# Attention and mixture-of-experts on one core: moving the tiny addition ahead of the softmax reciprocal from GpSimd to VectorE, from the third attention stage on

## The chip, the cores and the metric

One core of one Trainium2 chip. The metric is the device time of one execution in microseconds (us). The profile shows TensorE as PE (matmuls) and PEld (weight loads), VectorE as DVE, ScalarE as ACT, GpSimd as POOL, and SyncE, which issues the DMAs here, as SP.

## What is computed

```python
scores = scale * np.matmul(q, k.transpose(0, 1, 3, 2))     # 4 batches, 8 heads, 576 x 576, head size 64
kth = np.partition(scores, -32, axis=-1)[..., -32:-31]
scores = np.where(scores >= kth, scores, -1e9)
attn = np.exp(scores - scores.max(-1, keepdims=True))
attn = attn / (attn.sum(-1, keepdims=True) + 1e-09)
x = attn @ v                                                # laid out as 2304 rows of 512
P = np.exp(x @ w_gate - max)                                # 2304 x 8, eight rounds of row and column scaling
out = sum(P[:, e:e+1] * (np.maximum(x @ w1[e], 0) @ w2[e]) for e in range(8))
```

All in float32. The `1e-09` in the fifth line is the addition that the change moves.

## The kernel before, in words

The program has two halves that run interleaved on the same engines. Attention goes through the seven entries of `STAGES`; an entry is a batch with one or two blocks of 256 query rows, over four pairs of heads. The expert layer is computed for blocks of rows as soon as their attention is done, and its matmuls (lines 446 and 559) fill TensorE while attention goes on. When all attention is done, `sinkhorn` scales the gate matrix, and the last four blocks are computed together from line 671 and line 730 on.

One attention step of a head pair goes as follows. TensorE computes scores (lines 122 and 123) into one PSUM tile; ScalarE copies them to `s` (line 128); VectorE finds the 32 largest of each row by four maxima and three replacements (lines 138 and 141); GpSimd subtracts two of these numbers (line 142, `eb`); ScalarE raises the kept weights with two activations (lines 144 and 145), the second of which adds up the row sums into `st`. Then `normalise` runs: GpSimd adds 1e-9 to the sums (line 171), VectorE takes the reciprocal (line 172), and GpSimd (line 175) or ScalarE (line 177) multiplies the weights `Et` by it. Two row tiles of two heads go into one `st` of 128x2; the mixed rests of two batches (`rest_weights`) have an `st` of 128x1.

From the third stage on the weights are turned by a DMA: ScalarE splits `Et` into 16-bit halves (line 158, `halves`), SP transposes them (line 162, `turned`), and ScalarE joins them into `at` (line 165). The join is put in the program behind the next split, not behind its own. TensorE then multiplies `at` by the values (line 247; "the weigh" below: ten instructions in the program, twenty in the trace), and ScalarE copies the result to `xt` (line 270).

The expert layer splits each weight tile into a high part (`wh`, ScalarE, line 83) and a low part (`wl`, GpSimd, line 86), multiplies (line 446), stores the hidden layer as `hh` (ScalarE, line 514) and `hl` (VectorE, line 515), and multiplies again (line 559).

Nobody wrote the order of the instructions out: a list scheduler places every instruction in its engine's queue by priority (attention before experts) and by its own estimate of when the operands are there. Each engine then runs its queue strictly in that order. So an edit of one line can change the order of everything behind it. In `normalise`, `X` is the dictionary of finished row tiles: it has 2 entries in the first stage, 4 in the second and 6 in the third.

Of the kernel before, what the change touches and what calls it, by code (L numbers as in the profile page):

```python
# [11 lines left out]
OP = mybir.AluOpType  # L12
# [39 lines left out]
def kernel(  # L52
# [11 lines left out]
    nc = tc.nc  # L64
# [49 lines left out]
    X = {}  # L114
# [53 lines left out]
        turning.append(whole)  # L168

    def normalise(Et, st, n, on_pool=False):  # L170
        nc.gpsimd.tensor_scalar(st[:, 0, 0:n], st[:, 0, 0:n], 1e-9, 1.0, op0=OP.add, op1=OP.mult)
        nc.vector.reciprocal(st[:, 1, 0:n], st[:, 0, 0:n])
        for i in range(n):
            if on_pool:
                nc.gpsimd.tensor_scalar(Et[:, i, :], Et[:, i, :], st[:, 1, i:i + 1], 1.0, op0=OP.mult, op1=OP.mult)
            else:
                nc.scalar.activation(Et[:, i, :], Et[:, i, :], AF.Copy, scale=st[:, 1, i:i + 1])
# [41 lines left out]
    def weight_tiles(qs, ks, put, on_pool=False, crossed=None):  # L219
        for t in range(2):  # L220
            Et = ap_.tile([128, 2, S], F32, name="Et", bufs=2)
            st = ap_.tile([128, 2, 2], F32, name="st", bufs=3)
            units = []
            for i in range(2):
                o = i * 256 + t * 128
                qc = qs[:, o:o + 128]
                sp = scores([((a, 0, 288), [(qc, ks[i], slice(a * 288, a * 288 + 288))]) for a in range(2)])
                units.append((copy_scores(sp[:, :, 0:288]), Et[:, i, :], st[:, 0, i:i + 1]))
            topk(units, crossed is not None)
            normalise(Et, st, 2, on_pool)  # L230
            cs = slice(t * 128, (t + 1) * 128)
            if crossed is not None:
                cross(Et, crossed[:, :, cs])
                continue
            Ef = Et.rearrange("p a b -> p (a b)")
            for g in range(3):
                ps = pst.tile([128, 4, 128], F32, name="pt")
                for r in range(3):
                    j = g * 3 + r
                    nc.tensor.transpose(ps[:, r, :], Ef[:, j * 128:j * 128 + 128], idt)  # L240
                put(slice(g * 3, g * 3 + 3), cs, ps[:, 0:3, :])
# [37 lines left out]
    def rest_weights(qm, ks, put):  # L279
        Et = ap_.tile([128, 2, S], F32, name="Et", bufs=2)  # L280
        st = ap_.tile([128, 2, 2], F32, name="st", bufs=3)
        qa, qb = qm[:, 0:128], qm[:, 128:256]
        sp = scores([
            ((0, 0, 288), [(qa, ks[0], slice(0, 288)), (qb, ks[1], slice(64, 352))]),
            ((1, 0, 224), [(qa, ks[0], slice(288, 512)), (qb, ks[1], slice(352, 576))]),
            ((1, 224, 288), [(qa, ks[0], slice(512, 576)), (qb, ks[1], slice(0, 64))]),
        ])
        topk([(copy_scores(sp[:, :, 0:288]), Et[:, 0, :], st[:, 0, 0:1])])
        normalise(Et, st, 1)
        ps = pst.tile([128, 4, 128], F32, name="pt")  # L290
        for j in range(4):
            nc.tensor.transpose(ps[:, j, :], Et[:, 0, j * 128:(j + 1) * 128], idt)
        for i in range(2):
            put(slice(0, 128), slice(5 * i, 5 * i + 4), ps[:, :, i * 64:(i + 1) * 64])
        ps = pst.tile([128, 4, 128], F32, name="pt")
        nc.tensor.transpose(ps[0:64, 0, :], Et[:, 0, 512:576], idt)
        nc.tensor.transpose(ps[:, 1, :], Et[:, 0, 448:576], idt)
        for i, r in enumerate((va, vb)):
            put(r, 4, ps[r, i, r])
# [536 lines left out]
```

## Time and profile before

| | |
|---|---|
| median of 3 runs | 1862.87 us (1862.12 to 1863.7) |
| the profiled execution | 1861.39 us, of which its span is 1859.6 us |
| PE busy in the span | 1794.2 us, 96% |
| DVE, ACT, POOL busy | 65%, 63%, 56% |
| attention's last `normalise` (line 172) | at 1012.1 us |

Read the share of PE first: it is the engine that both halves need all the time. Then ask in which stretch the rest of its time lies; the profile's 40 slices show it mostly in the first eighth of the span.

### The profile page before, as it was taken

To read this page: it belongs to the slowest core of one execution; us is meant where nothing else is said; L and a number is where in the kernel's file an instruction comes from. 1 tells how busy PE (TensorE), PEld (TensorE's weight loads), DVE (VectorE), ACT (ScalarE), POOL (GpSimd) and SP (SyncE) were. 2 spreads that over 40 slices of the span, in tenths; PEclk is the share of its full clock that TensorE was granted. 3 is DMA by queue.
4 is the path that set the end of the run, shared out by engine and by line. 5 is a ranking of instruction groups with operands and counts; after the bars stand their busy time and mean duration, and the time that the engine had idled before them with its cause. 6 is when DMAs were issued, how large, how long until landed. Compare 5 with 4: busy or idle time off the path is not lost.

```text
span 1859.6 us, 26250 instructions
## 1 busy us (share of the span) xinstructions
PE 1794.2 (96%) x9361; PEld 1484.4 (80%) x9361; DVE 1208.9 (65%) x2235; ACT 1172.1 (63%) x1773; POOL 1047.8 (56%) x827
## 2 busy tenths in 40 slices
PE   4899998999999999999999999999999999999998
PEld 3778787878877878878877788888888888888886
DVE  8989988888888886978965231145555555533433
ACT  5888889898988987898888435433333333333331
POOL 3369755655655547565643948945554455555441
PEclk8999999999999999999999999999999999999999
DMA  4787766666556656565554337523333333311111
GB/s 128 237 286 237 218 173 186 203 169 165 165 144 167 173 135 198 155 160 162 165 134 112 105 131 227 185 85 111 117 110 117 103 102 108 97 62 59 56 35 45
DMA packets 212674, 266.17 MB, mean 143 GB/s; under 512 B 127424, under 2 KB 131648, under 8 KB 212544
## 3 DMA queue, kind: packets, MB, share of 16 engines
q1 hardware_dynamic: 212544, 264.51, 48.0%
q8 instruction: 73, 1.20, 0.3%
q14 instruction: 57, 0.47, 0.1%
HBM read 201.54 MB, written 34.60 MB: 127 GB/s over the span
## 4 chain that ended last, share of the span: by engine, by line
PE 73%; ACT 7%; DVE 6%; issue 5%; DMA 5%; POOL 4%; SPq 0%; ACTq 0%; POOLq 0%; DVEq 0%
PE p L730 19%; PE p L559 15%; PE p L446 14%; PE p L671 9%; PE pc L671 5%; DMA wr<-in_w_dram 3%; PE pt L247 3%; DVE m L138 3%; POOL wl L86 2%; PE pb L671 2%; DVE w L141 2%; PE sp L122 2%; PE sp L123 2%; ACT wh L83 1%; ACT at L165 1%
## 5 line engine op out<-in xcount | busy, mean ns | idle before, releaser
L86 POOL TENSOR_TENSOR wl<-wr,wh 128x1024 fp32r<-128x1024 f32 x280 | 675.1, 2420 | 509.9 <-ACT wh L83 500.1
L83 ACT ACTIVATE wh<-wr 128x1024 fp32r<-128x1024 f32 x280 | 295.1, 1060 | 281.9 <-PE p L671 191.6
L138 DVE MAX8 m<-w 128x8 f32<-128x576 f32 x432 | 321.8, 754 | 6.5
L446 PE MATMUL p<-xh,wh 128*128 128x256 f32 (+1 forms) x800 | 270.3, 338 | 1.5 <-DVE hl L515 1.5
L446 PE MATMUL p<-xh,wl 128*128 128x256 f32 (+1 forms) x800 | 268.4, 336 | 0.0
L446 PE MATMUL p<-xl,wh 128*128 128x256 f32 (+1 forms) x800 | 268.4, 335 | 0.0
L559 PE MATMUL p<-wh,hh 128*128 128x512 f32 x640 | 251.2, 397 | 4.7 <-ACT hh L514 4.5
L559 PE MATMUL p<-wl,hh 128*128 128x512 f32 x640 | 249.2, 392 | 0.0
L559 PE MATMUL p<-wh,hl 128*128 128x512 f32 x640 | 239.5, 391 | 0.0
L141 DVE MATCH_REPLACE8 w<-m,w 128x576 f32<-128x576 f32 x288 | 213.8, 743 | 0.0
L515 DVE SCALAR_TENSOR_TENSOR hl<-p,hh 128x512 fp32r<-128x512 f32 x160 | 109.0, 683 | 148.0 <-ACT hh L514 146.3
L730 PE MATMUL p<-wh,h2h 128*128 128x512 f32 x512 | 199.4, 389 | 1.3 <-ACT h2h L694 0.7
L730 PE MATMUL p<-wl,h2h 128*128 128x512 f32 x512 | 199.2, 389 | 0.0
L730 PE MATMUL p<-wh,h2l 128*128 128x512 f32 x512 | 196.4, 389 | 0.0
L576 DVE SCALAR_TENSOR_TENSOR acc<-p,P,acc 128x512 f32<-128x512 f32 x120 | 89.4, 749 | 160.9 <-PE p L730 160.9
L446 PEld LDWEIGHTS p<-xh,wh 128*128 128x128 f32 x800 | 152.4, 190 | 21.4 <-DVE hl L515 3.1
L446 PEld LDWEIGHTS p<-xh,wl 128*128 128x128 f32 x800 | 152.3, 190 | 15.7 <-issue 0.8
L446 PEld LDWEIGHTS p<-xl,wh 128*128 128x128 f32 x800 | 152.3, 190 | 15.5
L138 DVE MAX8 m<-s 128x8 f32<-128x576 f32 x144 | 108.2, 752 | 76.0 <-ACT s L128 75.3
L559 PEld LDWEIGHTS p<-wh,hh 128*128 128x128 f32 x640 | 120.6, 189 | 30.3 <-ACT hh L514 7.1
L559 PEld LDWEIGHTS p<-wl,hh 128*128 128x128 f32 x640 | 120.7, 189 | 23.0 <-POOL wl L86 0.2
L559 PEld LDWEIGHTS p<-wh,hl 128*128 128x128 f32 x640 | 119.8, 188 | 23.8 <-issue 0.4
(168 smaller groups left out, 3551.8 us busy)
## 6 DMA issues: line engine op xcount, KB each, us to landing
wr<-in_w_dram SPq DMA_DIRECT2D x240, 512.0 KB, 3.5
y<-y SPq DMA_DIRECT2D x160, 256.0 KB, 2.7
raw<-in_k_dram SPq DMA_DIRECT2D x56, 288.0 KB, 3.8
raw<-in_q_dram SPq DMA_DIRECT2D x32, 256.0 KB, 3.7
p<-y SPq DMA_DIRECT2D x32, 256.0 KB, 3.5
wr<-in_w_dram SPq DMA_DIRECT2D x32, 256.0 KB, 4.0
y<-p SPq DMA_DIRECT2D x32, 256.0 KB, 3.8
values<-in_v_dram SPq DMA_DIRECT2D x28, 256.0 KB, 3.1
```

The lines of the kernel that those rows point to most:

```text
L83: nc.scalar.activation(dst, src, AF.Copy)
L86: nc.gpsimd.tensor_tensor(dst, src, hi.bitcast(F32), op=OP.subtract)
L122: nc.tensor.matmul(o, qc, kh[:, cs], start=(i == 0), stop=False)
L138: nc.vector.max(m8[:, u, r, :], ws[u] if r else units[u][0])
L141: nc.vector.match_replace(ws[u], m8[:, u, r, :], ws[u] if r else units[u][0], LOWEST)
L247: weighed = nc.tensor.matmul(av[r, 0:n], vr[:, o:o + 64], at[:, block, 0:n], start=(j == order[0]), stop=(j == order[-1]))
L446: nc.tensor.matmul(ps[:, fo, :], a[:, kk, fs], x[:, k0 + kk, cs], start=(i == 0), stop=(i == 3 * nk - 1))
L515: nc.vector.scalar_tensor_tensor(seat.hl[:, ft, cs], src, 0.0, seat.hh[:, ft, cs].bitcast(F32), op0=OP.max, op1=OP.subtract)
L559: nc.tensor.matmul(ps, a[:, ft, ts], m[:, ft % 2, :], start=(i == 0), stop=(i == 3 * NFT - 1))
L576: return nc.vector.scalar_tensor_tensor(ACC[t], y, g, ACC[t], op0=OP.mult, op1=OP.add)
L671: nc.tensor.matmul(ps, w[:, kk, :], x[:, kk, :], start=(fresh and i == 0), stop=(i == 5), skip_group_check=True)
L730: nc.tensor.matmul(ps, a[:, ft, ts], m[:, ft, :], start=(i == 0), stop=(i == 11))
```

## The change

For every call of `normalise` in the third stage and behind it, the addition of 1e-9 is issued on VectorE, the engine that takes the reciprocal next. In the first two stages it stays on GpSimd. 64 of the 80 additions move: 48 of 128x2 and 16 of 128x1.

```diff
     def normalise(Et, st, n, on_pool=False):
-        nc.gpsimd.tensor_scalar(st[:, 0, 0:n], st[:, 0, 0:n], 1e-9, 1.0, op0=OP.add, op1=OP.mult)
+        adder = nc.vector if len(X) > 4 else nc.gpsimd
+        adder.tensor_scalar(st[:, 0, 0:n], st[:, 0, 0:n], 1e-9, 1.0, op0=OP.add, op1=OP.mult)
         nc.vector.reciprocal(st[:, 1, 0:n], st[:, 0, 0:n])
```

Behind the edit every line has a number higher by one, so line 172 of before is line 173 in the change, and the addition is line 172 there. The scheduler's order is the same up to the first moved addition and differs from there on all engines. Three places:

VectorE, at the first addition that moves, in the third stage (`m_1740` and `m_1809` are maxima of two row tiles). Before:

```order
L515 SCALAR_TENSOR_TENSOR hl<-p_3442,hh 128x2x256
L515 SCALAR_TENSOR_TENSOR hl<-p_3460,hh 128x2x256
L141 MATCH_REPLACE w<-m_1740,w 128x576
L138 MAX m_1809<-s 128x8
L138 MAX m_1740<-w 128x8
L172 RECIPROCAL st<-st 128x2
L141 MATCH_REPLACE w<-m_1809,s 128x576
```

With the change:

```order
L516 SCALAR_TENSOR_TENSOR hl<-p_3442,hh 128x2x256
L516 SCALAR_TENSOR_TENSOR hl<-p_3460,hh 128x2x256
L172 TENSOR_SCALAR st<-st 128x2
L141 MATCH_REPLACE w<-m_1740,w 128x576
L138 MAX m_1809<-s 128x8
L173 RECIPROCAL st<-st 128x2
L138 MAX m_1740<-w 128x8
L141 MATCH_REPLACE w<-m_1809,s 128x576
```

The addition stands two instructions ahead of the reciprocal, and the reciprocal one instruction earlier than before.

ScalarE, around the join (`at`) on which the eleventh weigh of the program waits (in the trace of before it starts at 300.84 us; `p_3917` is an expert result that is copied out just ahead). Before:

```order
L128 ACTIVATE s<-sp 128x576
L83 ACTIVATE wh<-wr 128x1024 x2
L144 ACTIVATE Et<-s,m_2145 128x576
L83 ACTIVATE wh<-wr 128x1024
L567 ACTIVATE y<-p_3917 128x512
L158 ACTIVATE halves<-Et 128x2304
L165 ACTIVATE at<-turned 128x9x256
L128 ACTIVATE s<-sp 128x576
L514 ACTIVATE hh<-p_3954 128x2x256
L514 ACTIVATE hh<-p_4011 128x2x256
```

With the change:

```order
L144 ACTIVATE Et<-s,m_2145 128x576
L568 ACTIVATE y<-p_3917 128x512
L515 ACTIVATE hh<-p_3976 128x2x256
L515 ACTIVATE hh<-p_3954 128x2x256
L128 ACTIVATE s<-sp 128x576
L83 ACTIVATE wh<-wr 128x1024 x2
L144 ACTIVATE Et<-s,m_2145 128x576
L158 ACTIVATE halves<-Et 128x2304
L165 ACTIVATE at<-turned 128x9x256
L128 ACTIVATE s<-sp 128x576
```

The store of `p_3954`, a copy of scores, a weight split and a weight activation (the second with `m_2145`) stood behind the join before and stand ahead of it now. Another split and another activation came in from ahead of the join in front, which changes nothing for this one.

TensorE, at the same weigh. Before:

```order
L446 MATMUL p_4011<-xh,wl 128x256
L122 MATMUL sp<-kh,qs 128x288
L123 MATMUL sp<-kl,qs 128x288
L122 MATMUL sp<-kh,qs 128x288
L123 MATMUL sp<-kl,qs 128x288
L247 MATMUL pt<-at,values 64x256 x10
```

With the change:

```order
L560 MATMUL p_4227<-wh,hh 128x512
L560 MATMUL p_4227<-wl,hh 128x512
L560 MATMUL p_4227<-wh,hl 128x512
L248 MATMUL pt<-at,values 64x256 x10
L122 MATMUL sp<-kh,qs 128x288
```

Between the weigh in front of this one and this one the queue holds 18 expert matmuls of line 446 and 48 of line 559 before, and 66 and 60 with the change.

Counted over TensorE's whole queue: at the thirteenth weigh and at the sixteenth (456.4 us in the trace) as many expert matmuls stand ahead as before, to within two. Between the sixteenth and the twenty-first weigh (629.36 us) there are 290 of line 446 and 324 of line 559 before, and 264 and 276 with the change. Ahead of the first matmul of `sinkhorn` there are 103 fewer. They are run behind it; the number of all matmuls is the same.

## Rows read from the trace of the kernel before

**Rows 1.** The page, part 1: busy time of each engine

```profile
PE 1794.2 (96%) x9361; PEld 1484.4 (80%) x9361; DVE 1208.9 (65%) x2235; ACT 1172.1 (63%) x1773; POOL 1047.8 (56%) x827
```

**Rows 2.** Busy time by stretch, first the stretch and its length

```profile
core 0: us, PE busy (x) PEld busy (x) DVE busy (x) ACT busy (x) POOL busy (x), PEclk, DMA share, GB/s
0.00:205.00 205.00, 166.31 (x959) 134.20 (x959) 192.21 (x403) 160.72 (x301) 121.69 (x120) 0.97 0.68 221
205.00:460.00 255.00, 239.15 (x1554) 204.35 (x1555) 223.82 (x441) 229.16 (x334) 149.41 (x138) 0.97 0.66 184
460.00:630.00 170.00, 169.09 (x859) 137.05 (x859) 139.68 (x273) 146.57 (x211) 97.43 (x85) 1.00 0.59 157
630.00:1012.00 382.00, 380.83 (x2038) 309.05 (x2033) 301.42 (x589) 327.32 (x492) 215.16 (x191) 1.00 0.57 157
```

**Rows 3.** Waits of PE from 205 to 1012: us, times, longest

```profile
PE pt L247 <- ACT at L165: 7.3, 2, 6.2
PE sp L122 <- ACT s L128: 6.2, 5, 1.9
```

**Rows 4.** PE timeline around 294 to 306: start, us, what, idle before

```profile
294.19 0.30 PE L122 MATMUL sp<-kh,qs 128*128 128x288 f32 x1
294.33 0.29 PE L123 MATMUL sp<-kl,qs 128*128 128x288 f32 x1
300.84 4.53 PE L247 MATMUL pt<-at,values 128*64 128x256 f32 x20 [6.22 <-ACT at L165]
305.31 0.61 PE L122 MATMUL sp<-kh,qs 128*128 128x288 f32 x1
...
306.43 0.52 PE L559 MATMUL p<-wh,hh 128*128 128x512 f32 x1
```

**Rows 5.** The stretch of 6 us behind that wait, columns as in rows 2

```profile
301.00:307.00 6.00, 6.00 (x26) 3.63 (x27) 5.54 (x11) 5.13 (x11) 3.51 (x4) 0.53 0.79 184
```

**Rows 6.** ACT timeline ahead of that weigh

```profile
288.31 0.76 ACT L145 ACTIVATE Et<-Et,eb 128x576 f32<-128x576 f32 x1
...
296.39 2.13 ACT L158 ACTIVATE halves<-Et 128x2304 uint16<-128x2304 uint16 x1
298.41 2.38 ACT L165 ACTIVATE at<-turned 128x2304 uint16<-128x2304 uint16 x1
```

**Rows 7.** Chain that ended last, two pieces: start, us, what

```profile
307.65 2.27 PE p L446 x19
...
338.91 5.47 PE p L559 x24
```

**Rows 8.** POOL's additions by shape: busy, mean ns, idle before

```profile
L171 POOL TENSOR_SCALAR st<-st 128x2 f32<-128x2 f32 x64 | 12.3, 192 | 64.8 <-ACT Et L145 61.9 <-POOL qs L86 0.2
...
L171 POOL TENSOR_SCALAR st<-st 128x1 f32<-128x1 f32 x16 | 3.1, 191 | 9.9 <-ACT Et L145 8.8
```

**Rows 9.** DVE timeline in the sinkhorn part: small instructions

```profile
1042.28 0.15 DVE L403 TENSOR_SCALAR nmx<-nmx 128x1 f32<-128x1 f32 x1
...
1043.29 0.18 DVE L414 TENSOR_SCALAR sp<-sp 128x18 f32<-128x18 f32 x1
1043.51 0.27 DVE L415 RECIPROCAL rs<-sp 128x18 f32<-128x18 f32 x1
```

**Rows 10.** Waits of DVE from 205 to 1012

```profile
DVE m L138 <- ACT s L128: 71.8, 40, 5.4
DVE st L172 <- POOL st L171: 23.8, 16, 4.8
```

**Rows 11.** Waits of POOL from 205 to 1012

```profile
POOL st L171 <- ACT Et L145: 49.3, 25, 6.4
```

**Rows 12.** The sixteenth weigh: ns min, median, max, first and last start

```profile
L247 PE MATMUL pt<-at,values x20: 432/432/483, 456.4 to 458.8; 128*64 128x320 f32 x20
```

**Rows 13.** PE timeline, the twenty-first weigh

```profile
629.36 2.38 PE L247 MATMUL pt<-at,values 128*64 128x256 f32 x20
```

**Rows 14.** ACT timeline, the join for that weigh

```profile
622.63 2.40 ACT L165 ACTIVATE at<-turned 128x2304 uint16<-128x2304 uint16 x1
```

## The prediction, made before the change was run

> **What bounds the kernel now.** I read the share of each engine first: PE is busy for 1794.2 of 1859.6 us [rows 1], so 65.4 us of the span are all that any better order can give back. Then the stretches [rows 2], to see where these 65.4 lie. The reader is to take length minus PE busy in each row: 38.7 us lie before 205, where the first two stages run and the order of every queue is unchanged; 15.85 lie between 205 and 460; 0.9 between 460 and 630; 1.2 between 630 and 1012; and the remaining 8.8 behind 1012, where attention is over. So the change can work on some 18 us. In the same rows VectorE is busy for 88% and ScalarE for 90% of 205 to 460, for 82% and 86% of 460 to 630, for 79% and 86% of 630 to 1012. GpSimd is never above 60%. In the first of the three stretches the attention chain is just about too slow for TensorE, in the other two TensorE is the bound and the chain has air.
>
> Then the waits of PE [rows 3]. One wait stands out: 6.2 us for the join of the turned weights. The timeline of PE [rows 4] shows it: the last score matmul starts at 294.33, the weigh at 300.84. On ScalarE the join starts at 298.41, at once behind the split of the next weights [rows 6]; ScalarE has been busy without a break since 288.31, so it is its queue that is late, not GpSimd's addition. The wait has an echo: in the 6 us behind it the granted clock is 0.53, mostly the lower of its two levels of 1.2 and 2.4 GHz [rows 5]. The weigh takes 4.53 us there [rows 4] against 2.38 for the same twenty instructions later [rows 13], 2.15 more. The four scores behind it take 1.12 (305.31 to 306.43) where a step is 0.14 otherwise (294.19 to 294.33), 0.56 more. The wait and its echo cost 6.2 + 2.7 = 8.9 us.
>
> **The instruction that moves.** GpSimd loses 64 additions of 192 and 191 ns [rows 8], 12.3 us, and the waits for the exponentials in front of them, 49.3 us in 25 cases [rows 11]. While it stood there, nothing behind it in its queue could start. Since GpSimd is idle 40% of the time and more, none of this is on the path that sets the end; I take 0 for it, covered by that idle time. VectorE gains 64 additions. Its trace has no 128x2 addition, so I bound it by near rows [rows 9]: a 128x1 multiplication took 0.15 us, and from a 128x18 addition to the dependent reciprocal behind it pass 0.22 us. That is 9.6 to 14.1 us; I take the upper one, because the moved addition too has a dependent reciprocal behind it, though mostly with two instructions in between. Against it stand the 23.8 us that VectorE waited at the reciprocal for GpSimd's addition [rows 10]. That wait doesn't vanish: VectorE now waits at its own addition for ScalarE's sums, in strict order, with the maxima of the next row tile queued behind. What goes is only GpSimd's 0.19 and its queue ahead of it. Below, nothing is gained; above, all of the 23.8; in sum I put VectorE's balance at zero, with -14 and +10 as ends, spread over 800 us.
>
> A page of the Trainium skill has a lower price: GPSIMD Engine Reference, section 8 (Key points), holds VectorE to be about twice as fast as GpSimd in elementwise work. By it an addition would be 96 ns (an estimate from that ratio and the 192 ns of the row) and all of them 6.1 us, and VectorE's share in the tight stretch below would come out about one point lower. The rows on VectorE's small instructions do not bear that out, 0.15 to 0.18 us against 0.19, and I go by them.
>
> **The order.** This is where the time is decided. At the late weigh TensorE's queue now holds 48 more matmuls of line 446 and 12 more of line 559 between the weigh in front and this one. A step of the former is 2.27/19 = 0.119 us, of the latter 5.47/24 = 0.228 [rows 7]: 5.7 + 2.7 = 8.4 us of other work. On ScalarE four instructions that stood behind the join are now ahead of it: a store of `hh`, a score copy, a weight split and a weight activation. Twelve such instructions take the 8.1 us from 288.31 to 296.39 [rows 6], 0.67 each, so the join comes 2.7 us later. The wait would be 6.2 + 2.7 - 8.4 = 0.5. So nearly all of the wait goes, and its echo with it: -5.7 - 2.7 = **-8.4 us**. Bounds: 0, if the extra matmuls have to wait for their own weights; and 15.85 + 2.7 = 18.6 if every wait of this stretch goes. I take the one wait, since it alone is seen to be filled.
>
> Between the sixteenth and the twenty-first weigh, TensorE loses 26 matmuls of line 446 and 48 of line 559. At 0.228 each (these are 512 wide) that is 16.8 us less filling, on the stretch from 456.4 [rows 12] to 629.36 [rows 13], 173 us. Attention is therefore asked to go through it in 156. For the window of 170 us in [rows 2] that means 153.2. The smaller filling takes some 2 us off ScalarE and 1.4 off VectorE (two stores, two copies); the additions (five weighs with up to three each) put 15 x 0.22 = 3.3 on VectorE. ScalarE would be busy for 144.6 of 153.2, 94%; VectorE for 141.6, 92%. Neither reached that in the dense stretch: 90% and 88%. At 90% ScalarE needs 160.7, that is 7.5 us more than TensorE's queue gives it. In hand is what the weighs have as lead today: the join was done at 622.63 + 2.40 = 625.03 [rows 14], the weigh started at 629.36, 4.3 us later. So TensorE waits 3.2 to 7.5 us more than now; I take the middle, **+5 us**. The bounds are 0 and the full 16.8.
>
> Behind 630 the order is pulled forward by another 6 us over 382; ScalarE's share goes from 86% to 87%. I cost it at nothing, hidden by that air; if it were gone, the price is those 6 us. The 23 us of matmuls (103 x 0.228) that move behind the sinkhorn part cost nothing in themselves: the number of matmuls is the same, and PE is the bound there.
>
> **The sum.** -8.4 + 5 = -3.4 us. Against the profiled execution of 1861.39 that is 1858.0, and that I predict; that execution is 1.5 us under the median of the runs shown, from which the same sum gives 1859.5. A measurement of this kernel can tell about 0.2%, 3.7 us, from no change, so the forecast lies right at that edge, and most of its own range is on the faster side.
>
> **The rivals.**
>
> *It comes back in full.* The wait at 294 goes, but attention doesn't get faster, and TensorE waits for it a little at many places between 310 and 630. For it: 88% and 90% in [rows 2] look like what this chain can do, and a chain that is late at one weigh by 6 us is late at the next. Against it: the leads of 4.3 us. Price: -8.4 + 8.4 = 0, 1861 to 1863. Chance 0.28.
>
> *Slower: ScalarE can't keep up from 456 on.* If ScalarE gets no more than the 86% it had in this stretch, it needs 144.6/0.86 = 168.1 us, 14.9 more than TensorE's queue allows. Waits of this size come in pieces of several us, and each such piece has the clock's echo, 2.7; with two of them, 14.9 + 5.4 - 8.4 = +11.9, 1873. It decides against the change from a share of 87.5% down (144.6/0.875 = 165.3: 12.1 us of wait, which eat up the 8.4 and the 3.7 that can be told). For it: VectorE's waits for score copies [rows 10] are waits for ScalarE's queue. Against it: part of those 71.8 us are waits because TensorE computed the scores late, and its queue now has them earlier. Chance 0.23.
>
> *Everything fits.* GpSimd, freed of 49.3 us of waiting in order, delivers the normalised weights earlier; the splits and joins come earlier; all waits between 205 and 460 go. -15.85 - 2.7 = -18.6, 1843. Chance 0.08.
>
> *Nothing happens at all*, because 64 additions of 0.2 us lie beside other work and the orders balance out: 1862. Chance 0.03. That the change doesn't do what it says can be left out: the queues show all 64 additions on VectorE.
>
> **How the numbers follow.** The forecast, -1 to -12 us, has the rest, 0.38. Faster by over 0.2%: 0.08 of the case where all fits, and 0.35 of the forecast, in all 0.43. Within 0.2%: 0.25 from the case that comes back, 0.03, and 0.03 from the forecast, in all 0.31. Slower: 0.23 and 0.03 from the case that comes back, 0.26. The range: below, it takes in the forecast and most of the way to the case where all fits, 1846; above, the slower case up to its 11.9 less a little, 1872. About one in ten is left out on each side. The forecast's own range is 1850 to 1861.
>
> **What would show it.** Right: the weigh near 300 us starts without a wait of several us, and the granted clock stays at 1.00 behind it; PE's idle time between 205 and 460 falls from 15.85 to 7 or less; between 460 and 630 it rises from 0.9 to about 6; the first matmul of sinkhorn comes 20 us or more earlier; VectorE's busy time rises by 10 to 14 us, GpSimd's falls by 12. Wrong: a new wait of PE of over 4 us at a weigh or a score between 310 and 630 with a clock under 1 behind it, which is the slower case; or PE's idle time between 205 and 460 as large as before at other places, which is the case that comes back. If PE idles less than 3 us in all from 205 to 1012, everything fits.

## The result: slower by about 10 us, and the profile after

The changed kernel took 1871.72 us (median of 6 runs, 1867.92 to 1877.31) against 1861.79 (6 runs, 1859.52 to 1863.7). The ratio is 1.0059, with a 95% interval of 1.0045 to 1.0074: 8 to 14 us slower. The forecast was 1858.0, so the sign is wrong. The time lies at the upper end of the range, near the 1873 of the slower rival, but it comes about in another way.

The profiled execution after took 1872.69 us, with a span of 1870.9. Part 1 of its page and the busy time by stretch, to set beside [rows 1, 2]:

```profile
PE 1800.7 (96%) x9361; PEld 1486.5 (79%) x9361; DVE 1225.9 (66%) x2299; ACT 1170.6 (63%) x1773; POOL 1035.9 (55%) x763
```

```profile
core 0: us, PE busy (x) PEld busy (x) DVE busy (x) ACT busy (x) POOL busy (x), PEclk, DMA share, GB/s
0.00:205.00 205.00, 166.69 (x964) 134.37 (x965) 193.20 (x406) 161.23 (x304) 122.93 (x122) 1.00 0.68 223
205.00:460.00 255.00, 239.32 (x1539) 204.23 (x1540) 228.44 (x458) 225.78 (x332) 144.02 (x114) 0.96 0.66 183
460.00:630.00 170.00, 165.65 (x858) 133.08 (x854) 149.49 (x302) 150.30 (x213) 94.69 (x76) 1.00 0.57 155
630.00:1012.00 382.00, 379.14 (x2002) 305.26 (x2004) 302.96 (x604) 325.21 (x490) 207.21 (x157) 0.99 0.56 156
```

TensorE is idle for 15.68 us between 205 and 460, as much as before (15.85), and for 4.35 between 460 and 630 (0.91 before). The waits of PE from 205 to 1012 now have other names than in [rows 3]:

```profile
PE p L560 <- ACT hh L515: 7.1, 6, 3.0
PE sp L122 <- ACT s L128: 5.4, 6, 2.6
PE p L560 <- ACT y L568: 4.3, 2, 3.2
...
PE pt L248 <- ACT at L165: 0.5, 1, 0.5
```

The wait of 6.22 us for the join [rows 4] is gone; the weigh there starts at 307.83 without one. But the matmuls that were put ahead of it wait instead, first for `hh`, then for `hl` (timeline of PE):

```profile
295.50 1.22 PE L560 MATMUL p<-wh,hh 128*128 128x512 f32 x2 [3.00 <-ACT hh L515]
298.28 0.58 PE L447 MATMUL p<-xh,wh 128*128 128x256 f32 x1 [1.55 <-DVE hl L516]
307.83 2.38 PE L248 MATMUL pt<-at,values 128*64 128x256 f32 x20
```

From 295 to 301, behind the 3.00 us in which TensorE stood, the granted clock is 0.50, the lower of its two levels (1.2 of 2.4 GHz). So the echo came along too.

Where the time went is read best from the starts of the weighs, since the same attention matmuls stand between two of them before and after. Columns are us between the starts of two weighs (8th, 16th, 21st and 24th of 36; the 8th starts at 211.5 before and 211.4 after):

| | before | after | matmuls of lines 446 and 559 in between |
|---|---|---|---|
| 8th to 16th | 244.8 | 247.3 | 2 more after |
| 16th to 21st | 173.0 | 156.6 | 74 fewer, 16.8 us |
| 21st to 24th | 94.4 | 102.5 | 4 more, 0.9 us |

The first stretch lost 2.5 us where 8.4 were to be gained. The second went through in 16.4 us less with 16.8 us less of expert matmuls, so it lost 0.4. The third took 8.1 us more with 0.9 more to do, so it lost 7.2. These make 10.1 of the 11.2 us by which the last part starts later (the first weight load of line 671, 672 after, at 1199.7 before and at 1210.9 after). From there to the end of the span it is 659.9 and 660.0.

The third stretch has one place that stands out (timeline of PE, then of ACT, after):

```profile
626.84 0.40 PE L447 MATMUL p<-xh,wl 128*128 128x512 f32 x1
630.47 0.79 PE L560 MATMUL p<-wh,hh 128*128 128x512 f32 x1 [3.23 <-ACT y L568]
```

```profile
621.54 0.65 ACT L128 ACTIVATE s<-sp 128x576 f32<-128x576 f32 x1
624.86 0.78 ACT L144 ACTIVATE Et<-s,m 128x576 f32<-128x576 f32 x1 [2.67 <-DVE m L138]
625.55 2.11 ACT L158 ACTIVATE halves<-Et 128x2304 uint16<-128x2304 uint16 x1
627.56 2.37 ACT L165 ACTIVATE at<-turned 128x2304 uint16<-128x2304 uint16 x1
629.84 0.58 ACT L568 ACTIVATE y<-p 128x512 f32<-128x512 f32 x1
```

TensorE waits for a result's PSUM buffer. The copy `y` that frees it stands on ScalarE behind a ramp (the weight activation of line 144), a split and a join, and the ramp waits 2.67 us for a maximum of VectorE. In the 6 us behind, from 631 to 637, the granted clock is 0.56, mostly the lower level.

### The profile page after: what moved, and what is told of

Same layout as the page of the kernel before. It is cut to its first block, busy times and chain, and to the rows that moved or that the text cites. A ratio compares the mean times of both kernels' runs of the same rounds, so it can differ in the third digit from the quotient of the medians.

```text
span 1870.9 us, 26351 instructions
## 1 busy us (share of the span) xinstructions
PE 1800.7 (96%) x9361; PEld 1486.5 (79%) x9361; DVE 1225.9 (66%) x2299; ACT 1170.6 (63%) x1773; POOL 1035.9 (55%) x763
## 4 chain that ended last, share of the span: by engine, by line
PE 63%; DVE 10%; ACT 10%; DMA 6%; issue 6%; POOL 4%; SPq 0%; ACTq 0%; POOLq 0%; DVEq 0%
PE p L731 19%; PE p L560 12%; PE p L447 10%; PE p L672 9%; DVE m L138 5%; PE pc L672 5%; DMA wr<-in_w_dram 4%; DVE w L141 4%; POOL wl L86 2%; ACT at L165 2%; PE pb L672 2%; PE pt L248 2%; ACT wh L83 2%; ACT halves L158 1%; DMA turned<-halves 1%
## 5 line engine op out<-in xcount | busy, mean ns | idle before, releaser
L447 PEld LDWEIGHTS p<-xl,wh 128*128 128x128 f32 x800 | 153.0, 191 | 16.4 <-issue 0.5
```

What stands on the lines that cost most here:

```text
L447: nc.tensor.matmul(ps[:, fo, :], a[:, kk, fs], x[:, k0 + kk, cs], start=(i == 0), stop=(i == 3 * nk - 1))
```

## The experiments

The scheduler sorts all queues anew at every edit, so the change is two things: an operation on another engine, and another order. To take them apart, most kernels here fix the order. The numbers that the program gives its instructions while it is written down are the same before and after. So a table of these numbers, per engine, can be laid over the program as edges that say issue order only:

```diff
     with _tile.TileContext(nc, schedule_with_timeline_sim=True) as tc:
         tile_topk_attention__then__sinkhorn_moe_kernel(tc, *args)
+        hold_order(tc)
...
+            if before is not None:
+                tc.add_manual_dep(now, before, after, reason="held order")
+            before = now.name
```

With the table of the kernel before this gives back its five queues, instruction for instruction. "Old" and "new order" below are the two tables. Holding an order has no price of its own that can be seen: `adds_late` below, in the old order with 33 of the 64 additions on GpSimd, takes as long as the kernel before. All ratios are to runs of the kernel before on the same chip, whose medians were 1860.6 to 1861.5.

**1. The operation without the order, and the order without the operation.** `op_alone` has the old order, with this one edit in VectorE's queue, 64 times (and the addition gone from GpSimd's):

```diff
+L172 TENSOR_SCALAR st<-st 128x2
 L173 RECIPROCAL st<-st 128x2
```

> The queues of all five engines are held to the order of the kernel before, instruction for instruction; the one difference is that the 64 additions stand in VectorE's queue, each directly ahead of its reciprocal, and not in GpSimd's. This is the operation without the new order. Theory ORDER (the 10 us come from the order into which the scheduler sorted the queues anew): as before within 4 us, 1858 to 1866. Theory OPERATION (64 more instructions on a VectorE that TensorE and ScalarE wait for cost the 10 us themselves): 1869 to 1875.

`order_alone` has the new order, with the 64 additions back on GpSimd (`adder = nc.gpsimd`).

> The queues are held to the order of the changed kernel, and only the 64 additions go back to GpSimd, at the place in the whole program where they stood. This is the new order without the operation. Theory ORDER: 1868 to 1876, as the changed kernel. Theory OPERATION: 1858 to 1865, as the kernel before. If each has a part of it, both this run and the one with the operation alone lie between, and their two differences add up to about 10 us.

Measured: 1865.94 us, ratio 1.0029 (1.0018 to 1.0040), for the operation; 1872.54, ratio 1.0060 (1.0046 to 1.0073), for the order. Both times lie in the ranges of ORDER, the first at its upper end. But the operation alone is clear of no change, by 5.3 us, and the two differences, 5.3 and 11.9, add up to 17 and not to 10. So neither theory is right as it was put.

**2. None, one and two additions.** `op_doubled` is `op_alone` with the addition twice:

```diff
         adder.tensor_scalar(st[:, 0, 0:n], st[:, 0, 0:n], 1e-9, 1.0, op0=OP.add, op1=OP.mult)
+        if len(X) > 4:
+            adder.tensor_scalar(st[:, 0, 0:n], st[:, 0, 0:n], 1e-9, 1.0, op0=OP.add, op1=OP.mult)
```

`op_dropped` has it in the first two stages only:

```diff
-        adder = nc.vector if len(X) > 4 else nc.gpsimd
-        adder.tensor_scalar(st[:, 0, 0:n], st[:, 0, 0:n], 1e-9, 1.0, op0=OP.add, op1=OP.mult)
+        if len(X) <= 4:
+            nc.gpsimd.tensor_scalar(st[:, 0, 0:n], st[:, 0, 0:n], 1e-9, 1.0, op0=OP.add, op1=OP.mult)
```

> As the run with the operation alone (order of the kernel before, additions on VectorE), with each of the 64 additions done twice, one behind the other; the sums so get 2e-9 and not 1e-9. Theory TIME (the 5 us of the operation alone are the time of 64 more instructions on VectorE): 5 us more, 1869 to 1873. Theory PLACE (they come from where VectorE now stands and waits, or from chance in the timing, and the 0.16 us of each addition are hidden): 1864 to 1868, as with one.

> The order of the kernel before with the 64 additions left out from the third stage on: the reciprocal takes the bare sums, and neither GpSimd nor VectorE adds the constant there. Theory TIME: the 5 us of the operation alone are gone, 1858 to 1862. Theory PLACE (the cost is that VectorE now waits for ScalarE's sums with no addition on another engine between): 1864 to 1868 still.

`new_dropped` has the same edit in the new order.

> The changed kernel's order with the 64 additions left out: the reciprocal takes the bare sums from the third stage on. In the order of before, none, one and two additions on VectorE gave 1860, 1866 and 1871.5. Theory TIME (an addition on VectorE costs as much in any order): 1864 to 1867. Rival HIDDEN (this order is bound elsewhere and was sorted with the additions in VectorE's queue, so they cost nothing in it): 1869 to 1874.

Measured: doubled 1871.50, ratio 1.0057 (1.0043 to 1.0071); dropped 1860.04, ratio 0.9991 (0.9982 to 1.0000); dropped in the new order 1866.69, ratio 1.0033 (1.0020 to 1.0046). That gives a table, medians in us:

| the 64 additions | none | on GpSimd | on VectorE | twice on VectorE |
|---|---|---|---|---|
| old order | 1860.0 | 1860.6 to 1861.5 | 1865.9 | 1871.5 |
| new order | 1866.7 | 1872.5 | 1871.7 | |

Theory TIME holds: by these medians each round of 64 additions on VectorE costs 5 to 6 us, in either order (5 to 7 by the ratios, each to its own chip). The new order costs 7 us even without them (8 by the ratios). And the same additions on GpSimd cost about 1 us, at the edge of what can be told, in the order that was sorted for them and 5 to 6 in the order that wasn't, which is why the two runs of the first part didn't add up.

The old order has the same matmuls on TensorE at the same places in all four of its runs, so the traces can be compared start by start. Between the starts of two weighs pass, from the 8th to the 21st, 414.1 us with none (209.68 to 623.74), 417.8 on GpSimd (211.53 to 629.36), 420.7 with one (211.58 to 632.32), 427.6 with two (208.75 to 636.32). From the 21st to the 36th it is 393.6, 393.5, 393.8 and 395.0, in the same sequence. So the price of the additions is paid ahead of 630 us. Single traces scatter, so small steps between them say little: from the 8th to the 21st weigh `adds_late`, which has these additions on GpSimd too, took 415.4 us and not 417.8, while `adds_early`, which has them on VectorE, took 420.8. One place, PE waiting for a score tile's copy near 233 us, with none, on GpSimd, with one and with two additions:

```profile
231.55 0.40 PE L122 MATMUL sp<-kh,qs 128*128 128x288 f32 x1 [1.58 <-ACT s L128]
```

```profile
233.50 0.40 PE L122 MATMUL sp<-kh,qs 128*128 128x288 f32 x1 [1.68 <-ACT s L128]
```

```profile
234.28 0.40 PE L122 MATMUL sp<-kh,qs 128*128 128x288 f32 x1 [2.41 <-ACT s L128]
```

```profile
232.56 0.61 PE L122 MATMUL sp<-kh,qs 128*128 128x288 f32 x1 [3.52 <-ACT s L128]
```

From none to one and from one to two additions the wait goes up by 0.8 and by 1.1 us. Behind it stands ScalarE, which has this copy in its queue behind a ramp that waits for VectorE's maxima (timeline of ACT, one addition):

```profile
226.12 0.78 ACT L144 ACTIVATE Et<-s,m 128x576 f32<-128x576 f32 x1 [0.68 <-DVE m L138]
...
233.59 0.64 ACT L128 ACTIVATE s<-sp 128x576 f32<-128x576 f32 x1
```

And VectorE's last maximum for this ramp stands behind an addition that took 2.35 us (timelines of POOL and of DVE, one addition):

```profile
218.37 4.90 POOL L86 TENSOR_TENSOR wl<-wr,wh 128x1024 fp32r<-128x1024 f32 x2 [4.76 <-ACT wh L83]
```

```profile
220.28 0.74 DVE L141 MATCH_REPLACE8 w<-m,w 128x576 f32<-128x576 f32 x1
220.95 2.35 DVE L172 TENSOR_SCALAR st<-st 128x2 f32<-128x2 f32 x1
223.33 0.17 DVE L173 RECIPROCAL st<-st 128x2 f32<-128x2 f32 x1
...
225.34 0.75 DVE L138 MAX8 m<-w 128x8 f32<-128x576 f32 x1
```

GpSimd's two subtractions for `wl` end at 223.27, the addition at 223.30. From the replacement in front of it to the last maximum pass 5.1 us; without additions it is 2.8 (219.49 and 222.33 in `op_dropped`). The addition was held up by GpSimd's instruction; how often this happens is counted in the next section.

**3. Which additions cost.** `adds_early` and `adds_late` split the 64 in the old order (`counted` is a counter of the calls from the third stage on; late has `> 33`):

```diff
-        adder = nc.vector if len(X) > 4 else nc.gpsimd
+        adder = nc.vector if len(X) > 4 and counted[-1] <= 33 else nc.gpsimd
```

> The order of the kernel before; of the 64 additions only the first 33, those ahead of the 21st weigh (629 us), go to VectorE, directly ahead of their reciprocals; the 31 behind stay on GpSimd. Theory PLACE (an addition costs where the weigh waits for the attention, which the traces of one and two additions show between 205 and 630 us alone): the whole 5 us, 1864.5 to 1867. Rival SHARE (each of the 64 costs the same): half of it, 1862 to 1864.

> The counterpart: the first 33 additions stay on GpSimd, the 31 behind the 21st weigh go to VectorE. Theory PLACE: nothing, 1859 to 1862, as before. Rival SHARE: 1863 to 1865.

Measured: early 1864.97, ratio 1.0027 (1.0017 to 1.0037); late 1861.49, ratio 1.0002 (0.9991 to 1.0012). The first 33 carry the whole price and the last 31 none: PLACE. The same instruction is free where TensorE hardly waits for attention (1.2 us idle in 382, [rows 2]), though the last 31 took 9.7 us of VectorE there.

**4. Where the order loses.** Two runs go over from one table to the other at the 16th weigh, one at the 24th; the additions are on VectorE in all three. The rows of each table were joined like this, for a place `k` in the first:

```diff
-rows = old
+rows = new[:k] + [i for i in old if i not in new[:k]]
```

> The changed kernel, held to its own order up to its 16th weigh (458.8 us), and behind that to the order of the kernel before for all that is left, each addition there directly ahead of its reciprocal. Theory LATE (the loss is made by the order behind 456 us, where the prediction put its charge of 5 us): 1855 to 1864, with the wait at 294 us gone as well. Theory EARLY (the loss is made between 205 and 456 us, by a slower clock and new waits that take back what the wait at 294 us had cost): 1868 to 1875.

> The counterpart: the order of the kernel before up to the 16th weigh (456.4 us), and the changed kernel's order for all that is left; the additions on VectorE throughout. Theory LATE: 1868 to 1876. Theory EARLY: 1858 to 1865.

> The changed kernel, held to its own order up to its 24th weigh (717.8 us), and behind that to the order of the kernel before; the run that went over at the 16th weigh (458.7 us) took 1865. Theory STRETCH (the order loses its time between the 16th and the 24th weigh, where it leaves TensorE 15 us less other work beside the same attention): 1869 to 1874. Rival SPREAD (the loss is spread over all that follows, to the end of the attention at 1000 us): 1865 to 1868.

Measured: 1865.12, ratio 1.0026 (1.0015 to 1.0036), for the new order up to the 16th weigh; 1875.67, ratio 1.0074 (1.0059 to 1.0089), for the new order behind it; 1871.22, ratio 1.0057 (1.0045 to 1.0069), for the new order up to the 24th. `new_then_old` takes as long as `op_alone`: the new order gains nothing and loses nothing ahead of the 16th weigh, the other wait at 294 us included. It lies just above the range of LATE, 1855 to 1864, which counted on a gain from that wait. Going on with the new order to the 24th weigh costs 6 us: STRETCH. And with the old order up to the 16th weigh the whole loss is there. So LATE holds for where the order loses its time, and not for the gain ahead of it. That `old_then_new` lies 4 us above the changed kernel is at the edge of what the intervals tell apart, and open.

**5. One wait of that stretch, mended by hand.** `copy_ahead` is the changed kernel with one row of ScalarE's queue moved:

```diff
+L568 ACTIVATE y<-p 128x512
 L144 ACTIVATE Et<-s,m 128x576
 L158 ACTIVATE halves<-Et 128x2304
 L165 ACTIVATE at<-turned 128x9x256
-L568 ACTIVATE y<-p 128x512
```

> The changed kernel, held to its own order, with one instruction moved: in ScalarE's queue the copy of a visit's result (y from p, at 629.84 us in the changed kernel's trace) goes ahead of the three instructions of the attention that stood before it (the ramp at 624.86, the split into halves, the join). Theory QUEUE (6 of the 10 us are lost there: TensorE stands 3.2 us at 627 for the buffer that this copy frees, then runs at a lower clock): 1864 to 1868. Theory FULL (ScalarE has too much to do in the whole stretch, so the copy that goes first only makes the join late): 1870 to 1874.

Measured: 1870.45, ratio 1.0049 (1.0035 to 1.0062), not to be told from the changed kernel. The wait is gone in its trace; the copy fits into the time in which ScalarE stood idle:

```profile
623.30 0.60 ACT L568 ACTIVATE y<-p 128x512 f32<-128x512 f32 x1 [1.57 <-PE p L560]
624.38 0.78 ACT L144 ACTIVATE Et<-s,m 128x576 f32<-128x576 f32 x1 [0.48 <-DVE m L138]
```

From the 21st weigh to the 24th it still took 100.3 us (614.9 to 715.2), 2.2 less than after and 5.9 more than before. The waits of PE over the whole of 205 to 1012 are 24.0 us in the sum of their groups, against 22.7 in the changed kernel. The time lies in the range of FULL. That speaks for it: the single wait is where the lateness shows, not what makes it.

**6. The wait at 294 us in the old order, cut by hand.** `join_ahead` takes the additions on GpSimd and moves split and join to the front on ScalarE, with the rows that depend on it, and four matmuls of TensorE behind others:

```diff
 L128 ACTIVATE s<-sp 128x576
+L158 ACTIVATE halves<-Et 128x2304
+L165 ACTIVATE at<-turned 128x9x256
+L144 ACTIVATE Et<-s,m 128x576
+L128 ACTIVATE s<-sp 128x576
+L567 ACTIVATE y<-p 128x512
 L83 ACTIVATE wh<-wr 128x1024 x2
...
```

> The kernel before, held to its own order, with the wait at 294 us cut by hand: ScalarE's split and join (296.39 and 298.41 us) go ahead of the two weight copies, the ramp, the third weight copy and the result's copy that stood before them, the scores' copy and two of hh follow at once, and on TensorE four matmuls of a visit go behind the 24 matmuls that followed them. Theory ORDER (single places in a queue decide a few us each): the weigh starts some 4 us earlier and 2 to 5 us are kept, 1856 to 1859. Theory FULL (what goes first only pushes the wait on to the next matmuls, as the changed order did at 292 and 295 us): 1860 to 1865.

`join_ahead_2` moves two rows more:

```diff
+L270 ACTIVATE xt<-pt 128x256
+L128 ACTIVATE s<-sp 128x576
 L83 ACTIVATE wh<-wr 128x1024
...
-L270 ACTIVATE xt<-pt 128x256
-L128 ACTIVATE s<-sp 128x576
```

> The run with the join ahead (order of the kernel before, additions on GpSimd), whose weigh started 4.9 us earlier and whose TensorE then stood 5.1 us at 303 us for the scores' copy, which ScalarE had behind a weight copy that waited 2.6 us for its transfer. Here the copy of the weigh's result and that copy of the scores go ahead of this weight copy too. Theory ORDER (each wait at this place is one instruction's place in a queue): 1857 to 1861. Rival FULL (ScalarE and VectorE have no room here, and the next wait takes its place): 1862 to 1866.

Measured: 1865.10, ratio 1.0019 (1.0010 to 1.0028); and 1865.61, ratio 1.0025 (1.0015 to 1.0035). The weigh did start earlier in the first (timeline of PE), and the next score matmul paid for it:

```profile
295.90 4.05 PE L247 MATMUL pt<-at,values 128*64 128x256 f32 x20 [2.94 <-ACT at L165]
...
308.33 0.61 PE L122 MATMUL sp<-kh,qs 128*128 128x288 f32 x1 [5.11 <-ACT s L128]
```

That is FULL again, the first run just above its range. Freeing that copy as well, in the second run, didn't help. The two orders were made by hand and push three weight splits back, so they show that this way of cutting the wait gains nothing, not that none could.

**7. Further ahead in VectorE's queue.** `op_spaced` has the old order with the additions on VectorE at the place in the program where GpSimd had them, for most of them like this:

```diff
+L172 TENSOR_SCALAR st<-st 128x2
 L138 MAX m<-w 128x8
-L172 TENSOR_SCALAR st<-st 128x2
 L173 RECIPROCAL st<-st 128x2
```

> The order of the kernel before with the additions on VectorE, as the run with the operation alone, but each at the place in the whole program where it stood on GpSimd, so that 47 of the 64 have one to four other instructions of VectorE between them and their reciprocal (25 have one), and 17 none. In the traces an addition directly ahead of its reciprocal holds VectorE's queue for 0.19 us, one with another instruction behind it for 0.12. Theory PITCH (what counts is how long the queue is held): 1863 to 1865.5. Rival EARLY WAIT (further ahead it stands waiting for ScalarE's sums with work behind it that was ready): 1866 to 1872.

Measured: 1869.27, ratio 1.0047 (1.0033 to 1.0061). It lies in the range of EARLY WAIT, and above `op_alone` by 3 us, which is just at the edge of the two intervals. So having something between an addition and its reciprocal saved nothing; that waiting for ScalarE's sums with maxima queued behind is what cost more is argued, not shown.

**8. Without the addition at all.** `no_adds` and `no_adds_free` delete the addition for all 80 calls, with the old order and without any.

```diff
-        nc.gpsimd.tensor_scalar(st[:, 0, 0:n], st[:, 0, 0:n], 1e-9, 1.0, op0=OP.add, op1=OP.mult)
         nc.vector.reciprocal(st[:, 1, 0:n], st[:, 0, 0:n])
```

> The order of the kernel before, with all 80 additions left out, those of the first two stages too; the reciprocal takes the bare sums. A sum holds the weight of its row's largest score, which is 1, and 1 + 1e-9 is 1 in float32. With the 64 left out it took 1860.0 beside 1861.5 before. Theory FREE (additions on GpSimd are nearly hidden): 1858 to 1861. Rival FIRST STAGES (ahead of 205 us TensorE stands 38 us, and each of the 16 additions there is a hand-over from ScalarE over GpSimd to VectorE on the way to the first weighs): 1852 to 1857.

> The same without the additions, but sorted by the scheduler as it likes. Theory ORDER (every edit sorts the queues anew, and what the new order is worth is larger than what 80 additions on GpSimd are): anywhere from 1852 to 1872, more than 3 us from the run above. Rival STABLE (the order of the kernel before comes back nearly whole): within 2 us of it.

Measured: held 1858.19, ratio 0.9994 (0.9983 to 1.0005); sorted anew 1867.06, ratio 1.0037 (1.0023 to 1.0051). In the old order 80 instructions fewer can't be told from before. Sorted anew the same program is 6 to 7 us slower than before, and 9 slower than in the old order: ORDER. Here work was only taken away, so the whole loss is the sorting's. No run gave a version that is shown to beat the kernel before.

## Why the prediction was wrong, step by step

**The reading of the bound held.** The time was lost where it said that time could be moved, between 205 and 1012, and the part behind the attention cost the same as before.

**"In sum I put VectorE's balance at zero": this step failed, on both of its sides.** The debit was mis-sized. Undisturbed, an addition next to its reciprocal holds the queue for 0.20 us, as these rows of `op_alone` show (start, us, what), inside the bounds of 0.15 to 0.22:

```profile
250.30 0.17 DVE L172 TENSOR_SCALAR st<-st 128x2 f32<-128x2 f32 x1 [0.82 <-ACT Et L145]
250.50 0.17 DVE L173 RECIPROCAL st<-st 128x2 f32<-128x2 f32 x1
```

But the mean is far above that (groups of `op_alone`: busy, mean ns, idle before):

```profile
L172 DVE TENSOR_SCALAR st<-st 128x2 f32<-128x2 f32 x48 | 23.2, 483 | 9.1 <-ACT Et L145 9.1
L172 DVE TENSOR_SCALAR st<-st 128x1 f32<-128x1 f32 x16 | 2.2, 140 | 7.6 <-ACT Et L145 7.6
```

Of the 48 additions of 128x2, 14 took longer than 0.25 us, up to 2.35, and each of them ends 0.02 to 0.03 us behind the end of a subtraction of GpSimd (line 86, which reads two tiles) that was running when it started. In the changed kernel it is 19 of 19. Those of 128x1 were not held: none took longer than 0.16 us, though nine started beside such a subtraction. So the 64 additions took 25.4 us of VectorE, 24.9 in the changed kernel, and not the 9.6 to 14.1 of the forecast. The rows that it took the price from [rows 9] are one of 128x1 and two on the PSUM tile `sp`, and show no such case.

The credit failed too. The 23.8 us of [rows 10] were put down to GpSimd's addition, but with no addition behind the second stage VectorE still waits at the reciprocal, now for ScalarE, and it waits longer for the copied scores, 76.1 us against 71.8 (waits of DVE, `op_dropped`, 205 to 1012):

```profile
DVE m L138 <- ACT s L128: 76.1, 48, 5.1
...
DVE st L173 <- ACT Et L145: 18.1, 6, 5.4
```

Of the 23.8 us 5.7 are gone by these traces, and 4.3 of them came back at another wait. Nor was the debit "spread over 800 us" without effect: the first 33 additions, 15.7 us of VectorE in `op_alone` and 12.2 of these in ten that were held, cost 4 to 5 us of the kernel (experiment 3). From 205 to 460 VectorE is busy for 88% of the time and ScalarE for 90% [rows 2], each waits for the other, and TensorE waits for both. That time added on one engine of such a loop reaches the end is argued from this; that two rounds cost twice as much fits it. How much of the price is made by the held additions no run tested. The starts of the weighs suggest a large part: from the 8th weigh to the 9th `adds_early` falls 2.4 us behind `op_dropped`, where held additions took 2.8 us, and from the 11th to the 14th by nothing, where seven additions stand of which none was held. The Trainium skill's lower price (GPSIMD Engine Reference, section 8, Key points: about half of GpSimd's time) isn't borne out for an operand this small: 0.13 to 0.17 us where nothing held it, against 0.19 on GpSimd [rows 8].

**The -8.4 for the wait at 294 failed altogether.** The wait did leave the weigh, with the 60 matmuls ahead of it, as forecast. But what came is the 0 of its bound, "if the extra matmuls have to wait for their own weights", only that they waited for `hh` and `hl`, 3.00 and 1.55 us, and the clock fell as before. ScalarE reached this `hh` at 294.37 us, after a queue without a break from 281.8 us on. VectorE, which makes `hl`, had just stood for a transfer, the first half's partial result (timeline of DVE, after):

```profile
293.08 0.70 DVE L511 TENSOR_TENSOR p<-p,y 128x512 f32<-128x512 f32 x1 [4.41 <-DMA y<-p]
```

All runs in the new order up to this place show this wait with 4.4 to 4.9 us, all in the old order with 0.7 to 1.1. No run moved the transfer, so what it costs is open. Without additions on either side the stretch from the 8th weigh to the 16th took 242.6 us in the old order (209.7 to 452.3) and 245.3 in the new (210.5 to 455.8); with the additions on VectorE, 246.9 (`op_alone`) and 247.3. So the order lost 0.4 to 2.7 us there. The rival "it comes back in full" was right here, with its own sign: PE's idle time from 205 to 460 as large as before, at other places. Experiment 6 agrees: a wait cut by hand in the old order comes back too.

**The +5 for the stretch with less filling: right in kind, one stretch too early and too small.** It was charged to the weighs from the 16th to the 21st. Those went through with a loss of 0.4 us, ScalarE 89% busy (139.6 of 156.6 us, from 458.8 to 615.4) and VectorE 88%. The charge fell due behind the 21st weigh (615 after, 629 before), on the part "behind 630" that the forecast cost "at nothing": 7.2 us up to the 24th weigh, 5.3 of them without any addition (`new_dropped`). In sum 7.6 against 5. The leads (from the end of a join to the start of its weigh) were used up in the first of the two stretches: the 21st weigh, 4.3 us behind its join before [rows 13, 14], now waits for it (timelines of ACT and PE, after):

```profile
612.91 2.39 ACT L165 ACTIVATE at<-turned 128x2304 uint16<-128x2304 uint16 x1
```

```profile
615.35 2.38 PE L248 MATMUL pt<-at,values 128*64 128x256 f32 x20 [0.46 <-ACT at L165]
```

The copy `y` is the first thing that was late by more. That the leads were what carried the first stretch is argued from the traces; no run tested it. The 23 us of matmuls that moved behind `sinkhorn` did cost nothing in themselves; `sinkhorn` began only 13 us earlier for them (the transpose at 1041.4 and 1028.3) and not 20.

**The sum.** Forecast: 0 for the operation, -8.4 and +5 for the order, -3.4. Measured: 5 to 6 for the operation (5.9 in the old order, 5.0 in the new, from the medians in the table) and 6 to 7 for the order (6.7 without additions, 5.8 with them on VectorE). The slower rival gave 1873 with -8.4 in it and 20 us of waits behind 456. Its mechanism is the one seen behind 615, but its number is met by accident.

## What to carry to other kernels

Where two engines wait for each other in turn at 88 and 90% and the third waits for both, an instruction of 0.2 us isn't covered by waits that its engine shows: ask whose lateness each wait passes on, for only what the removed hand-over itself adds can be saved. And price an instruction that moves to another engine beside what the other engines run there: an addition of 0.16 us took up to 2.35 us beside GpSimd's subtractions. Where a list scheduler sorts the queues, an edit is an operation and an order; hold the order to measure the first, and don't book a wait as gone until the work put into it is seen to be ready. A single late instruction in a stretch without air is a symptom: mend it by hand before believing that it is the cause.

## What the runs showed that was not expected

The recorded length of a VectorE instruction can hold a wait for another engine's instruction. The 48 additions of 128x2 are listed after with a mean of 468 ns, while those that nothing holds take 0.16 us (timeline of DVE, after):

```profile
207.27 2.23 DVE L172 TENSOR_SCALAR st<-st 128x2 f32<-128x2 f32 x1
...
405.86 0.16 DVE L172 TENSOR_SCALAR st<-st 128x2 f32<-128x2 f32 x1
405.97 0.76 DVE L138 MAX8 m<-w 128x8 f32<-128x576 f32 x1
```

The first did not wait for its operand, for ScalarE had the sums ready at 206.6 us. It ends at 209.50, just behind a subtraction of GpSimd that ends at 209.48. So of the 17.0 us by which VectorE's busy time rose, a part is waiting. The last two rows show the other thing: with an independent maximum behind it an addition holds the queue for 0.11 us, with its own reciprocal behind it 0.20.

And the size of chance in an order: the same program without the additions took 1858 us in the old order and 1867 sorted anew, a larger difference than the additions make on either engine.
